# First tiles by half features, interleaved loads, and first place for the up-projection's reads of PSUM, in a fused attention and feed-forward kernel

**Chip, cores, metric.** One core of one Trainium2 chip. The time is device microseconds of one execution; all runs here are in the fast state. A profile's span is 1.7 to 1.8 us shorter than the time of the same run, so spans are compared with spans and times with times.

## The reference

```python
h  = x + A(layernorm(x))          # x: 2048 x 1024, bf16
h2 = h + B(layernorm(h))
# A: 32 heads of 32; four segments of 512 tokens, one after the other
#    causal softmax attention inside the segment, plus a linear memory
#    (phi(q) M) / (phi(q) z) of the earlier segments, mixed by sigmoid(beta); then @ wo
# B: (silu(x @ w1) * (x @ w3)) @ w2, with 3584 hidden features
```

## The kernel before

The program builds some thousands of operations with costs and dependencies; a list scheduler in it then fixes one order per engine. Each operation has a class (`cls`, lower goes first), and a table SHIFT, tuned beforehand by search, nudges the operations of each unit. Weights stream through two buffers for each of `w1b` and `w3b`, so a load can start only when the last matmul that reads its buffer is done.

The parts that the change and the argument touch are the sixteen warm-up matmuls, the normalisation of the first four 128-token tiles (`ln_act` on ScalarE for tile 1, `ln` on VectorE for the others), the first projections, and the three reads of an up-projection's PSUM banks (`sg`, `t1`, `hm`):

```python
    def constants(self):
        P = self.pool_op
        i = self.ident[:, :]
        w = self.oT[0][:, 4, :]
        self.dve_op(lambda e: e.memset(w, 0.0), 300.0, [], [w], 0)
        gr = self.dense_group()
        wl = self.oT[0][:, 4, 0:128]
        self.mms(gr, [(lambda gr: self.bank(gr), wl, w, True, True, 512)] * 16, 0, split=16)
        # ... [cut: identity, masks, ones]

    def ln_act(self, k, src, dst):

        self.g.stage()
        sm, nm, sq = (self.lnst[:, k, i:i + 1] for i in range(3))
        junk = self.oT[0][:, 0:2, :].rearrange("p a b -> p (a b)")
        G = self.g
        G.op("act", act_ns(1024), lambda e, gr: [e.activation(junk, src, AF.Copy, accum_out=sm)],
             reads=[src], writes=[junk, sm], cls=1)
        self.act(nm, sm, AF.Copy, 190.0, cls=1, scale=-1.0 / 1024)
        G.op("act", act_ns(1024, 1), lambda e, gr: [e.activation(
            junk, src, AF.Square, bias=nm, accum_out=sq)], reads=[src, nm], writes=[junk, sq],
            cls=1)
        ve, rs = self.lnve[:, k:k + 1], self.rstd[:, k:k + 1]
        mh = self.mhalf[:, :]
        self.pool_op(lambda e: e.tensor_scalar(ve, sq, 1.0 / 1024, self.EPS, op0=ALU.mult,
                                               op1=ALU.add), 1, [sq], [ve], 0)
        self.pool_op(lambda e: e.tensor_tensor(rs, ve, mh, op=ALU.pow), 190, [ve, mh], [rs], 0)
        self.dve_op(lambda e: e.tensor_scalar(dst, src, nm, rs, op0=ALU.add, op1=ALU.mult),
                    540.0, [src, nm, rs], [dst], 0, port=True)

    def ln(self, k, src, dst, cls):

        self.g.stage()
        st = self.lnst[:, k, :]
        mv = self.lnmv[:, k, :]
        for c in range(2):
            a, b = self.lnst[:, k, 6 * c:6 * c + 6], src[:, c * 512:(c + 1) * 512]
            self.dve_op(lambda e, a=a, b=b: e.bn_stats(a, b), 630.0, [b], [a], cls - 1)
        st2 = self.lnst[:, k, :].rearrange("p (a b) -> p a b", a=2)
        self.dve_op(lambda e: e.bn_aggr(mv, st2), 200.0, [st2], [mv], cls - 1)
        ve, rs = self.lnve[:, k:k + 1], self.rstd[:, k:k + 1]
        var, mean = self.lnmv[:, k, 1:2], self.lnmv[:, k, 0:1]
        mh = self.mhalf[:, :]
        self.pool_op(lambda e: e.tensor_scalar(ve, var, self.EPS, None, op0=ALU.add), 1,
                     [var], [ve], 0)
        self.pool_op(lambda e: e.tensor_tensor(rs, ve, mh, op=ALU.pow), 190, [ve, mh], [rs], 0)
        self.dve_op(lambda e: e.tensor_scalar(dst, src, mean, rs, op0=ALU.subtract,
                                              op1=ALU.mult), 540.0, [src, mean, rs], [dst],
                    0 if k < 4 else cls, port=True)

    def ln1(self, s):
        for i in range(4):
            t = 4 * s + i
            x = self.xs[t % 4][:, :]
            self.g.dma(x, self.x2d[t * 128:(t + 1) * 128, :], cls=0 if s == 0 else 2)
            if t == 1:
                self.ln_act(t, x, x)
            else:
                self.ln(t, x, x, 2 if s == 0 else 4 + s)
            if s:
                self.g.dma_t(self.xnT[s][:, :, i * 128:(i + 1) * 128], x, 3)
                continue
            gr = Group([(6,), (7,), (4,), (5,)], safe=True)
            self.transposes(gr, [(c * 128, self.xs[t % 4][:, c * 128:(c + 1) * 128])
                                 for c in range(8)], 2 if s == 0 else 4)
            out = self.xnT[s][:, :, i * 128:(i + 1) * 128]
            self.evac(gr, out, 1024, lambda b: b.rearrange("p (k n) -> p k n", k=8), cls=1,
                      bf=True)

    def first_half(self):


        (wq, sq), (wk, sk), (wv, sv) = (self.weights(kind, 0) for kind in "qkv")
        self.g.dma(wq[:, :, 0:256], sq[:, :, 0:256], cls=1)
        self.g.dma(wk[:, :, 0:256], sk[:, :, 0:256], cls=1)
        self.g.dma(wq[:, :, 256:512], sq[:, :, 256:512], cls=1)
        self.g.dma(wk[:, :, 256:512], sk[:, :, 256:512], cls=1)
        self.g.dma(wv[:, :, :], sv, cls=1)
        x = self.xnT[0]
        work = [(w, i, Group([(6,), (7,), (4,), (5,)], safe=True))
                for w in (wq, wk) for i in range(2)]
        for c0 in range(0, 512, 128):
            for w, i, gr in work:
                self.g.stage()
                self.mms(gr, [(lambda gr, c0=c0: self.bank(gr, 0, 128, c0),
                               w[:, c, i * 128:(i + 1) * 128], x[:, c, c0:c0 + 128],
                               c == 0, c == 7, 128) for c in range(8)], 5, split=8, eager=True)
        for w, i, gr in work:
            self.g.stage()
            out = (self.qT if w is wq else self.kT)[0][:, i, :]
            self.evac(gr, out, 512, lambda b: b, cls=1)
        # ... [cut: copies of q and k, the second half, v]

    # ... in ffn_up, for each 128 columns and each 512 tokens:
                for gr, w in ((gg, w1), (gu, w3)):
                    self.mms(gr, [(lambda gr: self.bank(gr),
                                   w[:, c, jj * 128:(jj + 1) * 128], hT[:, c, :],
                                   c == 0, c == 7, 512) for c in range(8)], 7)
                self.g.op("act", act_ns(512), lambda e, gr, sg=sg: [e.activation(
                    sg, self.bank(gr), AF.Tanh, scale=0.5)], writes=[sg], cls=2, group=gg)
                self.g.op("dve", dve_ns(512), lambda e, gr, sg=sg, t1=t1: [
                    e.scalar_tensor_tensor(t1, sg, 1.0, self.bank(gr), op0=ALU.add,
                                           op1=ALU.mult)], reads=[sg], writes=[t1], cls=2,
                    group=gg)
                dst = self.hm[fc][:, tc * 512:(tc + 1) * 512]
                self.g.op("dve", dve_ns(512), lambda e, gr, t1=t1, dst=dst: [
                    e.scalar_tensor_tensor(dst, t1, 0.5, self.bank(gr), op0=ALU.mult,
                                           op1=ALU.mult)], reads=[t1], writes=[dst], cls=2,
                    group=gu)
```

The softmax here doesn't subtract the row's maximum and nothing guards it: scores larger than these inputs give would overflow.

## Time and profile before

| | before |
|---|---|
| time, median of 3 runs | 906.06 us (905.48 to 906.42) |
| span of the profiled run | 905.0 us (that run took 906.68) |
| TensorE busy | 98% |
| VectorE, ScalarE, GpSimd busy | 46%, 32%, 20% |

Two rows of the page in forty slices of 22.6 us each (busy tenths), for the engine and the transfers that the change touches:

```profile
DVE  4586657789676566643353321211343333431111
DMA  7949852564731267722342321013123222301110
```

Counting slices from 0, VectorE reaches nine tenths only in slice 9 (204 to 226 us), and the DMA engines in slices 1 and 3. Neither is a bound on average; what matters is where TensorE waits for one of them. The rest of the page is read in the prediction. A caution for every count of TensorE: this trace has 5476 matmul records beside 5564 weight loads, about one in sixty missing. Sums over the whole span are corrected for that below.

### The profile page before, as it was taken

What the parts mean: (1) busy time and instruction counts of PE and PEld (TensorE: products, weight loads), DVE (VectorE), ACT (ScalarE), POOL (GpSimd) and SP (SyncE); (2) the same over time, 40 slices, a digit from 0 to 9 for tenths busy, and PEclk for the clock granted to TensorE, in tenths of its full rate; (3) what the DMA queues carried; (4) which work ended last, traced back from release to release, by engine and by line L of the source; (5) the groups of instructions that cost most, each with busy time, mean ns of one, the idle gap of its engine ahead of it and who ended that gap; (6) DMA issues with size and microseconds to landing.
All of it is one profiled execution on the core that took longest, in us unless ns stands there. A gap on an engine that the chain in (4) does not pass through costs nothing.

```text
span 905.0 us, 12909 instructions
## 1 busy us (share of the span) xinstructions
PE 890.9 (98%) x5476; PEld 409.4 (45%) x5564; DVE 420.5 (46%) x643; ACT 285.2 (32%) x299; POOL 179.9 (20%) x248
## 2 busy tenths in 40 slices
PE   8999999999999999999999999999999999999998
PEld 5444443434444344444444444444444444444445
DVE  4586657789676566643353321211343333431111
ACT  5768657685685721111111100000121111110000
POOL 2554538456374431000000000000000000000000
DMA  7949852564731267722342321013123222301110
GB/s 233 233 133 284 202 175 98 136 153 99 184 102 48 58 223 209 210 68 60 101 121 78 98 72 45 24 47 93 47 76 93 70 59 58 94 24 41 36 40 30
DMA packets 146473, 96.27 MB, mean 106 GB/s; under 512 B 45424, under 2 KB 133616, under 8 KB 146416
## 3 DMA queue, kind: packets, MB, share of 16 engines
q1 hardware_dynamic: 146416, 95.45, 37.9%
q8 instruction: 44, 0.72, 0.3%
q14 instruction: 13, 0.11, 0.0%
HBM read 76.55 MB, written 8.39 MB: 94 GB/s over the span
## 4 chain that ended last, share of the span: by engine, by line
PE 96%; DMA 2%; issue 1%; DVE 1%; ACT 0%; SPq 0%; POOL 0%; ACTq 0%
PE ps L706 89%; PE ps L1054 4%; PE ps L1009 3%; DMA wp<-in_A_wv_dram 1%; DMA xs<-in_A_x_dram 1%; DMA pkn<-pk 1%; ACT et L1021 0%; DVE hm L1179 0%; DVE t L1174 0%; SPq L297 0%; PE ps L718 0%; DVE oT L1125 0%; DVE R L1122 0%; DVE lnst L827 0%; ACT sg L1171 0%
## 5 line engine op out<-in xcount | busy, mean ns | idle before, releaser
L706 PE MATMUL ps<-hnT,w1b 128*128 128x512 bf16 x875 | 219.1, 379 | 1.3 <-issue 0.3
L706 PE MATMUL ps<-hnT,w3b 128*128 128x512 bf16 x882 | 216.7, 379 | 2.2 <-DVE hm L1179 1.5
L1171 ACT ACTIVATE sg<-ps 128x512 bf16<-128x512 f32 x112 | 66.9, 597 | 431.6 <-PE ps L706 431.6
L706 PE MATMUL ps<-w2b,hm 128*128 128x512 bf16 (+1 forms) x905 | 196.5, 372 | 1.0
L1174 DVE SCALAR_TENSOR_TENSOR t<-sg,ps 128x512 bf16<-128x512 bf16 x112 | 76.7, 685 | 194.3 <-ACT sg L1171 194.2
L1021 ACT ACTIVATE et<-ps 128x2048 bf16<-128x2048 f32 x80 | 149.9, 1874 | 31.2 <-PE ps L1009 30.9
L706 PEld LDWEIGHTS ps<-w2b,hm 128*128 128x128 bf16 x924 | 90.4, 98 | 103.3
L706 PEld LDWEIGHTS ps<-hnT,w3b 128*128 128x128 bf16 x896 | 87.2, 98 | 106.9 <-DMA w3b<-in_B_w_dram 1.9
L706 PEld LDWEIGHTS ps<-hnT,w1b 128*128 128x128 bf16 x896 | 87.1, 98 | 105.9 <-issue 8.2
L1030 POOL TENSOR_SCALAR_AFFINE_SELECT et<-et 128x512 bf16<-128x512 bf16 (+1 forms) x96 | 82.1, 862 | 93.0 <-ACT et L1021 93.0
L1179 DVE SCALAR_TENSOR_TENSOR hm<-t,ps 128x512 bf16<-128x512 bf16 x112 | 76.6, 686 | 46.0 <-PE ps L706 43.6
L1203 DVE TENSOR_TENSOR ob<-hr,ps 128x512 bf16<-128x512 bf16 (+1 forms) x33 | 22.1, 671 | 135.8 <-PE ps L706 135.8
L706 PE MATMUL ps<-wo,oT 128*128 128x512 bf16 x248 | 61.4, 379 | 0.7 <-issue 0.5
L706 PE MATMUL ps<-hnT,wp 128*128 128x512 bf16 x248 | 59.7, 380 | 0.9 <-issue 0.6
L706 PE MATMUL ps<-xnT,wp 128*128 128x512 bf16 (+1 forms) x344 | 59.6, 320 | 0.9 <-issue 0.6
L833 POOL TENSOR_SCALAR lnve<-lnmv 128x1 f32<-128x1 f32 x31 | 8.7, 284 | 167.8 <-DVE lnmv L829 167.7
L706 PEld LDWEIGHTS ps<-xnT,wp 128*128 128x128 bf16 x352 | 27.8, 98 | 25.0 <-issue 2.8
L706 PEld LDWEIGHTS ps<-wo,oT 128*128 128x128 bf16 x256 | 24.0, 98 | 29.3 <-issue 2.4
L706 PEld LDWEIGHTS ps<-hnT,wp 128*128 128x128 bf16 x256 | 23.5, 98 | 29.1 <-issue 3.6
L1108 DVE STREAM_TRANSPOSE R<-Rc 128x1024 f32<-128x1024 f32 (+1 forms) x32 | 35.0, 1099 | 0.3
L1009 PE MATMUL ps<-qT,kT 32*128 32x128 bf16 (+3 forms) x512 | 31.7, 301 | 0.3 <-ACT et L1021 0.2
L706 PE MATMUL ps<-wp,xnT 128*128 128x512 bf16 x122 | 30.3, 380 | 0.7 <-issue 0.6
(82 smaller groups left out, 567.5 us busy)
## 6 DMA issues: line engine op xcount, KB each, us to landing
w3b<-in_B_w_dram SPq DMA_DIRECT2D x28, 512.0 KB, 4.0
w1b<-in_B_w_dram SPq DMA_DIRECT2D x28, 512.0 KB, 3.8
wp<-in_A_wv_dram SPq DMA_DIRECT2D x8, 1024.0 KB, 7.3
wp<-in_A_wq_dram SPq DMA_DIRECT2D x7, 1024.0 KB, 5.3
wp<-in_A_wk_dram SPq DMA_DIRECT2D x7, 1024.0 KB, 5.4
w2b<-in_B_w_dram SPq DMA_DIRECT2D x7, 1024.0 KB, 7.2
xs<-in_A_x_dram SPq DMA_DIRECT2D x16, 256.0 KB, 5.4
h<-in_A_x_dram SPq DMA_DIRECT2D x16, 256.0 KB, 3.2
```

What stands on the lines that cost most here:

```text
L706: return [e.matmul(p[0](gr), p[1], p[2], start=p[3], stop=p[4]) for p in part]
L833: self.pool_op(lambda e: e.tensor_scalar(ve, var, self.EPS, None, op0=ALU.add), 1, [var], [ve], 0)
L1009: ins.append(e.matmul(self.bank(gr, j, 512 - 128 * kc, off), k[r, g0 + g, 128 * kc:128 * kc + 128], q[r, g0 + g, 128 * kc:512], start=True ...
L1021: return [e.activation(et[:, :, :], src, AF.Exp, scale=self.scale)]
L1030: self.pool_op(lambda e, v=v, pat=pat: e.affine_select(v, v, pattern=pat, compare_op=ALU.is_ge, fill=0.0, base=0, channel_multiplier=-1), ...
L1054: ins.append(e.matmul(self.ps[32 * j:32 * j + 32, b * 512 + 128 * kc:(b + 1) * 512], lhsT(i, kc, j), at[i, kc][:, j, :], start=kc == 0 and ...
L1108: sp = self.dve_op(lambda e, dst=dst, src=src: e.transpose(dst, src), dve_ns(512 * nr), [Rc[:, i, 0:nr, :]], [rs], 1)
L1171: self.g.op("act", act_ns(512), lambda e, gr, sg=sg: [e.activation(sg, self.bank(gr), AF.Tanh, scale=0.5)], writes=[sg], cls=2, group=gg)
L1174: e.scalar_tensor_tensor(t1, sg, 1.0, self.bank(gr), op0=ALU.add, op1=ALU.mult)], reads=[sg], writes=[t1], cls=2,
L1179: e.scalar_tensor_tensor(dst, t1, 0.5, self.bank(gr), op0=ALU.mult, op1=ALU.mult)], reads=[t1], writes=[dst], cls=2,
L1203: self.g.op("dve", dve_ns(n), lambda e, gr, hs=hs, ob=ob, n=n: [e.tensor_tensor(ob, hs, self.bank(gr, 0, n), op=ALU.add)], reads=[hs], wri ...
```

## The change

The intent: let TensorE start on real work earlier. Tile by tile, the normalisation, the transposes and the copies out of PSUM go by halves of 512 features, the copies on VectorE and ScalarE in turn; tiles 1 and 3 take their statistics on ScalarE, tiles 0 and 2 on VectorE; the first loads are interleaved (two tiles, half of wq, two tiles, half of wk). The three reads of the up-projection's banks get the highest class. The scheduler's costs are corrected and SHIFT is searched anew, so the order of everything moves.

```diff
[cut: SHIFT, the table of offsets and priorities of some 490 units, retuned as a whole]
@@ -563,7 +559,7 @@
 
 
 def pool_ns(n, inputs=1):
-    return 170.0 + n * (0.88 if inputs == 1 else 2.1)
+    return 210.0 + n * (0.88 if inputs == 1 else 2.1)
 
 
 def mm_ns(n):
@@ -753,15 +749,23 @@
             self.queues[b] = g
         return g
 
+    def warm(self, n, deps=()):
+
+        w = self.oT[0][:, 4, :]
+        gr = Group([(3,)])
+        o = self.mms(gr, [(lambda gr: self.bank(gr), self.oT[0][:, 4, 0:128], w, True, True,
+                           512)] * n, 0, split=n)
+        o.cost["pe"] *= 2
+        for d in deps:
+            self.g.dep(o, d)
+
 
     def constants(self):
         P = self.pool_op
         i = self.ident[:, :]
         w = self.oT[0][:, 4, :]
         self.dve_op(lambda e: e.memset(w, 0.0), 300.0, [], [w], 0)
-        gr = self.dense_group()
-        wl = self.oT[0][:, 4, 0:128]
-        self.mms(gr, [(lambda gr: self.bank(gr), wl, w, True, True, 512)] * 16, 0, split=16)
+        self.warm(10)
         P(lambda e: e.memset(i, 1.0), 128, [], [i], 0)
@@ -797,64 +801,77 @@
         self.dve_op(lambda e: e.tensor_scalar(gc, gc, 0.5, 0.5, op0=ALU.mult, op1=ALU.add),
                     dve_ns(8), [gc], [gc], 3)
 
-    def ln_act(self, k, src, dst):
+    def ln_act(self, k, src):
+
 
         self.g.stage()
-        sm, nm, sq = (self.lnst[:, k, i:i + 1] for i in range(3))
+        sm, nm, sq, nb = (self.lnst[:, k, i:i + 1] for i in range(4))
         junk = self.oT[0][:, 0:2, :].rearrange("p a b -> p (a b)")
         G = self.g
-        G.op("act", act_ns(1024), lambda e, gr: [e.activation(junk, src, AF.Copy, accum_out=sm)],
-             reads=[src], writes=[junk, sm], cls=1)
-        self.act(nm, sm, AF.Copy, 190.0, cls=1, scale=-1.0 / 1024)
-        G.op("act", act_ns(1024, 1), lambda e, gr: [e.activation(
-            junk, src, AF.Square, bias=nm, accum_out=sq)], reads=[src, nm], writes=[junk, sq],
-            cls=1)
+        G.op("act", act_ns(1024) + 190, lambda e, gr: [e.activation(
+            junk, src, AF.Copy, accum_out=sm)], reads=[src], writes=[junk, sm], cls=1)
+        self.act(nb, sm, AF.Copy, 203.0, cls=1, scale=-1.0 / 32768)
+        G.op("act", act_ns(1024, 1) + 190, lambda e, gr: [e.activation(
+            junk, src, AF.Square, bias=nb, scale=1.0 / 32, accum_out=sq)], reads=[src, nb],
+            writes=[junk, sq], cls=1)
+        self.act(nm, sm, AF.Copy, 203.0, cls=1, scale=-1.0 / 1024)
+        return sq, nm, ALU.add
[cut: ln split into ln_stats and ln; the costs of POOL operations spelled out]
+    def first_tile(self, t):
+
+        x = self.xs[t][:, :]
+        var, mean, op = self.ln_act(t, x) if t % 2 else self.ln_stats(
+            t, x, 1, (self.applied,) if t else ())
+        rs = self.rstd[:, t:t + 1]
+        ve, mh = self.lnve[:, t:t + 1], self.mhalf[:, :]
+        self.dve_op(lambda e: e.tensor_scalar(ve, var, self.EPS, None, op0=ALU.add), 70.0, [var],
+                    [ve], 0)
+        self.g.op("pool", 570.0, lambda e, gr: [e.tensor_tensor(rs, ve, mh, op=ALU.pow)],
+                  reads=[ve, mh], writes=[rs], cls=0)
+        for b in range(2):
+            xb = self.xs[t][:, 512 * b:512 * b + 512]
+            self.applied = self.dve_op(lambda e, xb=xb: e.tensor_scalar(xb, xb, mean, rs, op0=op,
+                                                                     op1=ALU.mult),
+                                       290.0, [xb, mean, rs], [xb], 0, port=True)
+            gr = Group([(0,), (1,), (2,)], safe=True)
+            self.transposes(gr, [(c * 128, self.xs[t][:, 512 * b + c * 128:512 * b + c * 128 + 128])
+                                 for c in range(4)], 2)
+            out = self.xnT[0][:, 4 * b:4 * b + 4, t * 128:(t + 1) * 128]
+            if t == 0 and b:
+                self.warm(1, [self.g.ops[-1]])
+            self.evac(gr, out, 512, lambda v: v[:, 0:512].rearrange("p (k n) -> p k n", k=4),
+                      cls=1, bf=True, engs=("dve", "act"))
 
     def ln1(self, s):
         for i in range(4):
             t = 4 * s + i
-            x = self.xs[t % 4][:, :]
-            self.g.dma(x, self.x2d[t * 128:(t + 1) * 128, :], cls=0 if s == 0 else 2)
-            if t == 1:
-                self.ln_act(t, x, x)
-            else:
-                self.ln(t, x, x, 2 if s == 0 else 4 + s)
-            if s:
-                self.g.dma_t(self.xnT[s][:, :, i * 128:(i + 1) * 128], x, 3)
-                continue
-            gr = Group([(6,), (7,), (4,), (5,)], safe=True)
-            self.transposes(gr, [(c * 128, self.xs[t % 4][:, c * 128:(c + 1) * 128])
-                                 for c in range(8)], 2 if s == 0 else 4)
-            out = self.xnT[s][:, :, i * 128:(i + 1) * 128]
-            self.evac(gr, out, 1024, lambda b: b.rearrange("p (k n) -> p k n", k=8), cls=1,
-                      bf=True)
+            x = self.xs[i][:, :]
[cut]
@@ -896,20 +913,25 @@
 
 
         (wq, sq), (wk, sk), (wv, sv) = (self.weights(kind, 0) for kind in "qkv")
-        self.g.dma(wq[:, :, 0:256], sq[:, :, 0:256], cls=1)
-        self.g.dma(wk[:, :, 0:256], sk[:, :, 0:256], cls=1)
-        self.g.dma(wq[:, :, 256:512], sq[:, :, 256:512], cls=1)
-        self.g.dma(wk[:, :, 256:512], sk[:, :, 256:512], cls=1)
-        self.g.dma(wv[:, :, :], sv, cls=1)
+        dma = self.g.dma
+        loads = [(self.xs[t][:, :], self.x2d[t * 128:(t + 1) * 128, :]) for t in range(4)]
+        loads.insert(2, (wq[:, :, 0:256], sq[:, :, 0:256]))
+        loads.insert(5, (wk[:, :, 0:256], sk[:, :, 0:256]))
+        loads += [(wq[:, :, 256:512], sq[:, :, 256:512]), (wk[:, :, 256:512], sk[:, :, 256:512]),
+                  (wv[:, :, :], sv)]
+        for out, in_ in loads:
+            dma(out, in_, cls=0)
+        for t in range(4):
+            self.first_tile(t)
         x = self.xnT[0]
-        work = [(w, i, Group([(6,), (7,), (4,), (5,)], safe=True))
+        work = [(w, i, Group([(5,), (6,), (7,), (4,)], safe=True))
                 for w in (wq, wk) for i in range(2)]
         for c0 in range(0, 512, 128):
             for w, i, gr in work:
                 self.g.stage()
                 self.mms(gr, [(lambda gr, c0=c0: self.bank(gr, 0, 128, c0),
                                w[:, c, i * 128:(i + 1) * 128], x[:, c, c0:c0 + 128],
-                               c == 0, c == 7, 128) for c in range(8)], 5, split=8, eager=True)
+                               c == 0, c == 7, 128) for c in range(8)], 5, split=4, eager=True)
         for w, i, gr in work:
             self.g.stage()
             out = (self.qT if w is wq else self.kT)[0][:, i, :]
[cut: a POOL cost, and one transpose of the attention from class 1 to 2]
@@ -1169,15 +1191,15 @@
                                    w[:, c, jj * 128:(jj + 1) * 128], hT[:, c, :],
                                    c == 0, c == 7, 512) for c in range(8)], 7)
                 self.g.op("act", act_ns(512), lambda e, gr, sg=sg: [e.activation(
-                    sg, self.bank(gr), AF.Tanh, scale=0.5)], writes=[sg], cls=2, group=gg)
+                    sg, self.bank(gr), AF.Tanh, scale=0.5)], writes=[sg], cls=0, group=gg)
                 self.g.op("dve", dve_ns(512), lambda e, gr, sg=sg, t1=t1: [
                     e.scalar_tensor_tensor(t1, sg, 1.0, self.bank(gr), op0=ALU.add,
-                                           op1=ALU.mult)], reads=[sg], writes=[t1], cls=2,
+                                           op1=ALU.mult)], reads=[sg], writes=[t1], cls=0,
                     group=gg)
                 dst = self.hm[fc][:, tc * 512:(tc + 1) * 512]
                 self.g.op("dve", dve_ns(512), lambda e, gr, t1=t1, dst=dst: [
                     e.scalar_tensor_tensor(dst, t1, 0.5, self.bank(gr), op0=ALU.mult,
-                                           op1=ALU.mult)], reads=[t1], writes=[dst], cls=2,
+                                           op1=ALU.mult)], reads=[t1], writes=[dst], cls=0,
                     group=gu)
 
     def ffn_down(self, blk):
[cut: the call of ln1(0) removed]
```

## The prediction

> **What bounds the kernel now.** I read four views in this order: the page (who is busy), the waits of TensorE, the timeline of the places where TensorE stood still, and the landing times of the first loads.
>
> The page first: the busy line, the busy row of PE by slices, and the head of the chain that ended last.
>
> ```profile
> PE 890.9 (98%) x5476; PEld 409.4 (45%) x5564; DVE 420.5 (46%) x643; ACT 285.2 (32%) x299; POOL 179.9 (20%) x248
> ...
> PE   8999999999999999999999999999999999999998
> ...
> PE 96%; DMA 2%; issue 1%; DVE 1%; ACT 0%; SPq 0%; POOL 0%; ACTq 0%
> ```
>
> TensorE is the bound everywhere except in the first slice and the last. Busy is not the same as peak, so I checked the pitch: the starts of the 128x512 matmuls are 0.216 us apart from 322.9 us to 902.4 us, in pieces of 10.79 us, with one record missing in each piece and only 0.37 us lost in all. That stretch is the feed-forward block, and nothing in it can be gained. What is left is the opening, a few waits in the attention stretch (20 to 322 us), and the tail after the last matmul (905.0 - 902.4 = 2.6 us, which the change doesn't touch).
>
> The second view, waits of TensorE from 13.5 to 322 us (columns: total us, times, longest):
>
> ```profile
> PE ps L706 <- issue: 2.5, 16, 0.2
> PE ps L706 <- DVE hm L1179: 1.5, 1, 1.5
> PE ps L706 <- DMA wp<-in_A_wv_dram: 0.3, 1, 0.3
> PE ps L706 <- DMA pkn<-pk: 0.2, 1, 0.2
> PE ps L706 <- DVE R L1122: 0.2, 1, 0.2
> PE ps L1009 <- ACT et L1021: 0.2, 1, 0.2
> ```
>
> "issue" is the gap at a switch between full and tiled matmuls, about 0.1 us each, and there are 80 score blocks before and after. One wait stands out, 1.5 us for the second read of an up-projection's PSUM bank. The timeline of VectorE at that place:
>
> ```profile
> 300.09 0.75 DVE L1122 SCALAR_TENSOR_TENSOR R<-ps,gcol,R 128x512 f32<-128x512 f32 x1
> 300.88 0.85 DVE L1125 TENSOR_TENSOR oT<-R 128x512 bf16<-128x512 f32 x1
> 301.65 0.68 DVE L1174 SCALAR_TENSOR_TENSOR t<-sg,ps 128x512 bf16<-128x512 bf16 x1
> 302.26 0.70 DVE L927 TENSOR_SCALAR phe<-phe 128x1024 bf16<-128x1024 bf16 x1
> 302.89 0.67 DVE L1179 SCALAR_TENSOR_TENSOR hm<-t,ps 128x512 bf16<-128x512 bf16 x1
> ```
>
> TensorE finished its score block at 302.04 and had no free bank until hm was written at 303.57. VectorE did oT and phe first, which free no bank.
>
> The third view, the opening on TensorE (start, length, what):
>
> ```profile
> 1.24 6.22 PE L706 MATMUL ps<-oT 128*128 128x512 bf16 x16 [1.24 <-DVE oT L761]
> 7.36 0.62 PE L718 MATMUL ps<-ident,xs 128*128 128x128 bf16 x8
> 9.23 0.62 PE L718 MATMUL ps<-ident,xs 128*128 128x128 bf16 x8 [1.25 <-DVE xs L817]
> 9.68 1.06 PE L706 MATMUL ps<-xnT,wp 128*128 128x128 bf16 x16
> 10.89 0.62 PE L718 MATMUL ps<-ident,xs 128*128 128x128 bf16 x8
> 11.35 1.95 PE L706 MATMUL ps<-xnT,wp 128*128 128x128 bf16 x32
> 13.13 0.61 PE L718 MATMUL ps<-ident,xs 128*128 128x128 bf16 x8
> ```
>
> Sixteen warm-up matmuls, then four tiles transposed one by one, then a stream. To turn the opening into one number I subtract from a time in the stream the useful work done by then (0.056 us per 128-wide, 0.216 per 512-wide matmul). The first score block starts at 19.86, after 32 transposes, 112 narrow and 12 wide matmuls: 1.79 + 6.25 + 2.59 = 10.63. So the opening costs 9.2 us.
>
> The fourth view, landing events of the loads, last of the 16 parts: x tiles at 3.44, 4.46, 6.13 and 7.41 us, first half of wq 9.15, first half of wk 10.82, second halves 12.51 and 14.16, wv 18.48. The transfers run at 290 GB/s without a pause, so a load's landing goes with the bytes queued before it.
>
> **What the Trainium skill says.** "TensorE: Matmul & The Clock Gate", Part 1: the array is at half clock until it has been busy for a window of about 3.4 us, and falls back after an idle one; 426.7 ns per cold wide matmul against 215.7 warm. The trace agrees: 0.427 us apart until about 6.4 us, 0.216 afterwards. "DMA: Bandwidth & Descriptors", "Issuing engines are not separate DMA queues" and "Queues, rings and completion order": on each DMA engine descriptors are taken in ring order. The trace agrees: landings are in issue order. So interleaving loads moves arrivals, not the sum. "VectorE: DVE Perf Modes", the errata section: each instruction has a fixed latency, so halves cost more than a whole. The trace has bf16 128x1024 applications at 0.54 us; no half of it is in this trace.
>
> **The change part by part.**
> 1. Up-projection reads of PSUM get the highest priority. In the stretch above, 0.70 us (phe) and 0.85 us (oT) no longer come before the reads. The wait was 1.5; I book -1.4. In the dense stretch one gap of 0.15 us goes: -0.1. The rest of that stretch has no gap to save, though its VectorE and ScalarE rows all change.
> 2. The opening. Warm-up falls from 16 to 10 plus 1, ending near 1.24 + 10 x 0.427 = 5.5 us. This saves nothing itself: the first tile wasn't ready by then. Loads now go x0, x1, wq half, x2, x3, wk half; by bytes wq half lands near 7.4, x2 near 8.3, x3 near 9.15 and wk half again at 10.82. Tile 0: landed 3.44, statistics to 4.75, aggregate to 5.1, the added epsilon on VectorE to 5.3, power on POOL (0.57) to 6.0, halves applied at 6.3 and 6.6, transposed and copied by about 7.4 and 8.0. First real matmuls near 7.5 instead of 9.68. But only the 16 with wq and tile 0 can go. Tile 1 has its first copy on ScalarE, behind the sum of tile 3, which waits for x3 at 9.15: 1.06 + 0.19 + 0.60 gives 11.0. At 11.1 TensorE has done 16 transposes and 16 matmuls, 1.8 us of work, so the opening stands at 9.3. From there 40 narrow matmuls are ready (2.2 us, to 13.3). On VectorE the epsilon of tile 3 stands before the application of tile 2, and waits for ScalarE's square: 11.05 + two small operations of 0.2 + 1.15 + 0.19 gives 12.85. Tile 2 is then applied by 13.35 and 13.65, tile 3 by 14.1 and 14.4, and their copies end by 16.0 while TensorE has old work between. I find 0.25 us of holes. Opening: 9.5 against 9.2, +0.3. The early start is eaten by a longer idle time, because wk half lands no earlier.
> 3. The retuned order of everything. Work on TensorE is the same but for the five warm-up matmuls; one more block of tiled attention matmuls is split, two switches, +0.2. The space between score blocks must hold one exp (1.87 us) and its handshakes. Before, three spaces have 2.37 us of matmuls or less, and two of them cost 0.2 each. The new order has eight such, +0.6 if they cost 0.1 to 0.2. Against it, the old waits for wv (0.48), for pkn (0.3) and the like, about 1 us in all, sit at places that a new order shuffles: -0.3.
> Sum: -1.5 + 0.3 + 0.2 + 0.6 - 0.3 = -0.7. That the costs in the scheduler's tables were brought near the trace (power 0.57, epsilon, the accumulator read 0.19) speaks for a somewhat better order than my count, so I take -1.3: 904.8 us.
>
> **The rivals.**
> A. The opening really gets shorter, by 1.5 to 2 us (to 902.5 to 903.5). For: first matmuls 2 us earlier, epsilon off POOL, copies on two engines. Against: wk half at 10.82 caps what can be done, and the copy of tile 1 stands behind a landing.
> B. The clock stays cold. With busy time ending at 5.5 and tile 0 at 6.4, the window that ends near 6.4 is about three quarters busy. If that isn't enough, the 128-wide work goes at 0.107 until the next window, 9.8 or 13.2: up to +1.5 us, to 907. For: the removed matmuls were the ones that made that window full. Against: one warm-up was put back, and TensorE is waiting for data then anyway.
> C. A new wait takes the place of the removed one: VectorE serves the up-projection first and is late with the attention's eviction or a normalised tile, 1 to 3 us, to 906 to 908. For: VectorE is 9.09 us busy of 10 from 290 to 300. Against: four reads of 0.69 us only.
>
> **Range and chances.** All of the gain must come out of some 9 us of opening and 4 us of waits; even all waits and 2 us of opening are 6 us, 0.7%. So over 2% either way is next to impossible. A: 0.3, B or C: 0.3, near my sum: 0.4. Predicted 904.8, 8 in 10 between 902.3 and 907.4; faster by 2% 0.01, within 0.98, slower 0.01.
>
> **What would show it.** First real matmul near 7.5 us; then TensorE idle until about 11; opening (as computed above) 9.5. No wait of TensorE for hm in the attention stretch. Dense stretch unchanged at 0.216. Waits for exp somewhat more in number. Wide matmuls at 0.427 or transposes 0.107 apart after 6.5 us would show B. If the opening is below 8.5, or a single new wait exceeds 1 us, my working is wrong there.

## The result

| | before | changed |
|---|---|---|
| time, median of 6 runs each, same chip | 905.85 us (905.48 to 906.77) | 905.81 us (905.46 to 905.98) |
| ratio of the means | | 0.9997, 95% interval 0.9985 to 1.0010 |
| span of the profiled run | 905.0 us | 904.1 us |

A ratio here is the mean time of one kernel's fast runs over the mean of the other's of the same rounds, so not quite the ratio of the medians. The change is worth nothing that can be measured. (Before's profiled run was one of its slower ones, so the 0.9 us between the spans flatters the change.)

The page of the changed kernel, the busy line and the head of the chain that ended last:

```profile
PE 897.7 (99%) x5559; PEld 409.7 (45%) x5559; DVE 427.7 (47%) x653; ACT 284.5 (31%) x303; POOL 186.7 (21%) x246
...
PE 97%; DMA 2%; DVE 0%; issue 0%; ACT 0%; POOL 0%; SPq 0%
```

PE's row of forty slices is the same as before's to the digit: the two places where TensorE can gain are still the first slice and single waits. The busy time rose by 6.8 us only because this trace lacks no matmul record: b_prio below, which has before's order and lacks none either, has 897.7 us too.

To see where time went I split each span in three: the opening (as the prediction computes it: start of the first score block minus the useful work before it), the waits of TensorE after that, and the rest (matmuls at full pitch, the switches between matmuls on the whole array and those on a part of it, the tail).

| us | before | changed |
|---|---|---|
| opening | 9.2 | 9.17 |
| waits after it | 2.8 | 1.62 |
| rest | 893.0 | 893.3 |
| sum, the span | 905.0 | 904.1 |

The waits of TensorE in the changed kernel (total us, times, longest), for the attention stretch from 13.5 to 322 us and, after the dots, from 322 us to the end:

```profile
PE ps L702 <- DMA wp<-in_A_wq_dram: 0.2, 1, 0.2
...
PE ps L702 <- DMA w3b<-in_B_w_dram: 0.9, 2, 0.5
```

The 1.5 us wait at 302 us is gone, as are the waits for wv and pkn. (Before's rows for "issue" and R are gone too, but they were no waits: b_prio, the same order with all records, has neither.) But the feed-forward stretch, in which before lost 0.37 us in all, now has two waits for a load of w3b. The timeline of TensorE at these (start, length, what, and in brackets the idle time before it):

```profile
484.44 1.90 PE L702 MATMUL ps<-hnT,w3b 128*128 128x512 bf16 x8 [0.39 <-DMA w3b<-in_B_w_dram]
...
627.57 1.90 PE L702 MATMUL ps<-hnT,w3b 128*128 128x512 bf16 x8 [0.51 <-DMA w3b<-in_B_w_dram]
```

Measured from start to start and less the pitch, they cost 0.55 and 0.67 us; the wait for wq at 27 us costs 0.39. That is 1.6 us, all three for DMA.

**The opening.** TensorE in the changed kernel:

```profile
6.61 1.01 PE L714 MATMUL ps<-ident,xs 128*128 128x128 bf16 x8 [0.93 <-DVE xs L856]
...
7.84 1.91 PE L702 MATMUL ps<-xnT,wp 128*128 128x128 bf16 x16
9.55 0.83 PE L714 MATMUL ps<-ident,xs 128*128 128x128 bf16 x8
10.84 2.41 PE L702 MATMUL ps<-xnT,wp 128*128 128x128 bf16 x40 [0.47 <-ACT xnT L725]
```

The first projection starts at 7.84 instead of 9.68 us. Behind its sixteen matmuls and the transposes of tile 1 TensorE has nothing until 10.84, while before took up tile 2 at 10.89. The sixteen matmuls from 7.84 take 1.91 us: they run 0.107 us apart, at half clock. The reason for the gap is on ScalarE:

```profile
8.93 1.06 ACT L811 ACTIVATE oT<-xs 128x1024 bf16<-128x1024 bf16 x1 [0.67 <-DMA xs<-in_A_x_dram]
9.89 0.19 ACT L811 ACTIVATION_READ_ACCUMULATOR oT<-xs 128x1 f32 x1
10.19 0.60 ACT L725 ACTIVATE xnT<-ps 128x512 bf16<-128x512 bf16 x1
```

The sum of tile 3 waits for its load, which landed at 8.91; the copy of tile 1, which TensorE needs, stands behind it and ends at 10.79.

**A second look at before.** The prediction put the 1.5 us at 302 us on VectorE's `hm`. Two lines of before's page, side by side, should have stopped me: the same matmuls, once as matmuls and once as weight loads (busy us, mean ns; then idle time before them and what ended most of it):

```profile
L706 PE MATMUL ps<-hnT,w3b 128*128 128x512 bf16 x882 | 216.7, 379 | 2.2 <-DVE hm L1179 1.5
...
L706 PEld LDWEIGHTS ps<-hnT,w3b 128*128 128x128 bf16 x896 | 87.2, 98 | 106.9 <-DMA w3b<-in_B_w_dram 1.9
```

And the timeline of weight loads at the place:

```profile
301.71 0.10 PEld L1009 LDWEIGHTS ps<-qT,kT 32*128 32x128 bf16 x4 [0.42 <-ACT sg L1171]
303.39 0.55 PEld L706 LDWEIGHTS ps<-hnT,w3b 128*128 128x128 bf16 x4 [1.58 <-DMA w3b<-in_B_w_dram]
```

The weight load waited 1.58 us for the DMA of w3b. That load was issued at 297.49; fifteen of its sixteen parts had landed by 302.14, the last at 303.35, 0.04 us before the weights were read. `hm` was still being written then (until 303.56); by the program's dependencies the bank of these matmuls had been freed by R, which ended at 300.84. Why, then, does the matmul line name `hm`?

```profile
303.62 0.81 PE L706 MATMUL ps<-hnT,w3b 128*128 128x512 bf16 x3 [1.51 <-DVE hm L1179]
```

It has x3 where there are four weight loads. The record of the first matmul is one of those missing from this trace; it would stand at 303.40 (303.62 less a pitch of 0.216), before the end of `hm`. What the line calls the first matmul is the second, and the last event before that one was `hm`. The weight load line names what held TensorE. The Trainium skill, page "DMA: Bandwidth & Descriptors", section "Why a DMA increments its semaphore by 16 and not by 1", says that the parts run on engines that finish independently and that only the full count means that all data has landed. The trace agrees: one part of sixteen, 1.21 us behind the others, held TensorE.

That left two theories for the wait at 302 us. **D (DMA), "Theory B" in the recorded expectations:** the wait is for the load; the priority of the reads does nothing, and the changed kernel's gain there was paid back at two other loads. **V (VectorE), the prediction's, "Theory A" there:** the reads, done late, hold the bank. And two for the opening: either the landing of the first loads sets it, or what the code can change does (clock, copy order, ScalarE).

### The profile page after: what moved, and what is told of

It is laid out like the page before. It is cut to its first block, busy times and chain, and to the rows that moved or that the text cites. A ratio compares the mean times of both kernels' runs of the same rounds, so it can differ in the third digit from the quotient of the medians.

```text
span 904.1 us, 12979 instructions
## 1 busy us (share of the span) xinstructions
PE 897.7 (99%) x5559; PEld 409.7 (45%) x5559; DVE 427.7 (47%) x653; ACT 284.5 (31%) x303; POOL 186.7 (21%) x246
## 4 chain that ended last, share of the span: by engine, by line
PE 97%; DMA 2%; DVE 0%; issue 0%; ACT 0%; POOL 0%; SPq 0%
PE ps L702 90%; PE ps L1076 4%; PE ps L1031 3%; DMA w3b<-in_B_w_dram 1%; DMA wp<-in_A_wq_dram 1%; DMA xs<-in_A_x_dram 0%; PE ps L714 0%; DVE lnst L825 0%; ACT xnT L725 0%; POOL rstd L852 0%; DVE xs L856 0%; DVE ob L1225 0%; DVE lnmv L828 0%; DVE lnve L850 0%; DVE blkmask L788 0%
## 5 line engine op out<-in xcount | busy, mean ns | idle before, releaser
L702 PE MATMUL ps<-hnT,w3b 128*128 128x512 bf16 x896 | 219.0, 379 | 0.9 <-DMA w3b<-in_B_w_dram 0.9
L1052 POOL TENSOR_SCALAR_AFFINE_SELECT et<-et 128x512 bf16<-128x512 bf16 x96 | 88.4, 927 | 81.7 <-ACT et L1043 81.6
L702 PE MATMUL ps<-wo,oT 128*128 128x512 bf16 x256 | 63.9, 380 | 0.0
L702 PE MATMUL ps<-xnT,wp 128*128 128x512 bf16 (+1 forms) x352 | 62.5, 326 | 0.7 <-ACT xnT L725 0.5
L702 PE MATMUL ps<-hnT,wp 128*128 128x512 bf16 x256 | 62.6, 380 | 0.0
L835 POOL TENSOR_SCALAR lnve<-lnmv 128x1 f32<-128x1 f32 x28 | 6.3, 228 | 150.8 <-DVE lnmv L828 150.7
L1135 POOL TENSOR_TENSOR R<-Nsb,R 128x512 f32<-128x512 f32 x20 | 26.7, 1341 | 34.9 <-DVE R L1130 26.7
L1165 DVE TENSOR_TENSOR h<-h,ps 128x512 bf16<-128x512 bf16 x32 | 21.9, 684 | 24.8 <-PE ps L702 24.7
```

Of the source, the lines that this page charges most:

```text
L702: return [e.matmul(p[0](gr), p[1], p[2], start=p[3], stop=p[4]) for p in part]
L1052: self.pool_op(lambda e, v=v, pat=pat: e.affine_select(v, v, pattern=pat, compare_op=ALU.is_ge, fill=0.0, base=0, channel_multiplier=-1), ...
L1135: self.either(lambda e, o1=o1, Ns=Ns, R0=R0: e.tensor_tensor(o1, Ns, R0, op=ALU.mult), 512, 2, [Ns, R0], [o1], 2)
L1165: self.g.op("dve", dve_ns(512), lambda e, gr, hs=hs: [e.tensor_tensor(hs, hs, self.bank(gr), op=ALU.add)], reads=[hs], writes=[hs], cls=1, ...
```

## The experiments

In every kernel below whose edit is a move, the scheduler's order is frozen and replayed, so that one move reshuffles nothing else. All gave correct results. "Before" ran beside them, with medians of 905.97, 906.83, 906.54 and 905.88 us in the four batches, which is the scatter between chips and calls: only ratios are compared across batches.

### b_swap: before, with the bank's reads ahead of the other VectorE work

```diff
  VectorE near 301 us, frozen order of before
  R
- oT
- t
- phe
- hm
+ t
+ hm
+ oT
+ phe
```

> The kernel before with its order of instructions frozen and one edit: near 302 us VectorE does the two reads of the up-projection (t, then hm) ahead of oT and phe. Theory A (the 1.5 us wait of TensorE is for the read hm, as the prediction had it): hm ends near 302.7 instead of 303.57, TensorE resumes near 302.8, the wait shrinks to about 0.7 us, span shorter by 0.8 us. Theory B (the wait is for the load of w3b, which landed at 303.35 in the trace of before, its 16 parts spread over 2.6 us; hm was only the last to come by the profile): TensorE resumes when w3b has landed, whatever VectorE does; where the load lands on time there is no wait at all; the edit itself is worth 0, time within 0.3 us of before.

Measured: 905.59 us, ratio 0.9996 (0.9984 to 1.0008). VectorE and then TensorE at the place:

```profile
301.47 0.69 DVE L1209 SCALAR_TENSOR_TENSOR hm<-t,ps 128x512 bf16<-128x512 bf16 x1
```

```profile
302.06 1.04 PE L736 MATMUL ps<-hnT,w3b 128*128 128x512 bf16 x4 [0.52 <-DMA w3b<-in_B_w_dram]
```

`hm` now starts 1.4 us earlier than in before (301.47 against 302.89; 0.85 of that against the score block ahead of it, 301.14 here and 301.71 there). The wait is still there, and now it bears its right name: w3b landed at 302.01 and TensorE went on at 302.06. `hm` itself ended at 302.16, after TensorE had gone on, so it did not hold the bank. The wait is shorter (0.52) because the last part of this load was less late (0.53 us behind the fifteenth, against 1.21), not because of VectorE; the next run shows that.

### b_prio: before, with the new classes alone

```diff
- sg: cls=2    t: cls=2    hm: cls=2
+ sg: cls=0    t: cls=0    hm: cls=0
```

> The kernel before with only the priority of the three up-projection reads raised, as in the change; the scheduler then places later work anew. Theory A: about -1.5 us in the profile, no TensorE wait over 1 us in the attention stretch. Theory B: the reads are worth nothing; the time stays within 0.7 us of before, and what waits TensorE has in the feed-forward stretch are for loads of w1 or w3.

Measured: 906.37 us, ratio 1.0007 (0.9992 to 1.0022). I compared the compiled order with before's: not one instruction moves on any engine. The priority change is a no-op in before's schedule, and this kernel is a repeat of before. In that repeat:

```profile
303.02 1.04 PE L706 MATMUL ps<-hnT,w3b 128*128 128x512 bf16 x4 [0.77 <-DMA w3b<-in_B_w_dram]
```

```profile
303.03 0.67 DVE L1179 SCALAR_TENSOR_TENSOR hm<-t,ps 128x512 bf16<-128x512 bf16 x1
```

TensorE went on at 303.02, before `hm` even began; w3b had landed at 302.97. With the same instructions the wait was 1.5 us in one run and 0.77 in another: it follows the load. Theory V is out, and D holds at this place.

### a_noprio: the changed kernel without the new classes

```diff
- sg: cls=0    t: cls=0    hm: cls=0
+ sg: cls=2    t: cls=2    hm: cls=2
```

> The changed kernel with the priority of the reads put back to what it was. Theory A: a wait for hm of about 1 us or more returns, +1 to +1.5 us. Theory B: within 0.7 us of the changed kernel, waits for loads of w3b of 0 to 1.3 us in all at other places.

Measured: 906.08 us, ratio to before 0.9997 (0.9985 to 1.0009), just the ratio of the whole change. The order differs from the changed kernel's in a few rows only (four operations of VectorE moved). No wait for `hm` came back; the waits of TensorE after 13.5 us are all loads:

```profile
PE ps L702 <- DMA w3b<-in_B_w_dram: 0.6, 2, 0.4
PE ps L702 <- DMA wp<-in_A_wq_dram: 0.3, 1, 0.3
```

So the wait at 302 us went because the new order issues that w3b at 296.46 and it landed at 300.11, ahead of its use, not because of the classes.

### a_warm16: the changed kernel with sixteen warm-up matmuls again

```diff
- self.warm(10)
+ self.warm(16)      # the cost in the scheduler left at that of 10, so the order stays
```

> The changed kernel with 16 warm-up matmuls emitted instead of 10, all else in the same order. Theory of the cold clock (rival B of the prediction, as seen in the trace after: narrow matmuls 0.107 us apart until about 9.9 us): they are 0.056 apart from about 6.6 us, the transposes of tile 1 end near 9.1 instead of 10.2. But the first copy of tile 1 waits on ScalarE behind the sum of tile 3 (landing at 8.9), so TensorE resumes at 10.8 all the same: opening within 0.2 us of 9.2, time within 0.4 us of the changed kernel. If the cold clock is what costs, the opening falls by 0.5 us or more.

Measured: 905.45 us, ratio 0.9989 (0.9977 to 1.0000). TensorE in the opening:

```profile
8.06 1.07 PE L702 MATMUL ps<-xnT,wp 128*128 128x128 bf16 x16 [0.22 <-DMA wp<-in_A_wq_dram]
...
11.10 2.41 PE L702 MATMUL ps<-xnT,wp 128*128 128x128 bf16 x40 [1.35 <-ACT xnT L725]
```

The sixteen projections run at full clock here, 1.07 us instead of 1.91, yet TensorE resumed at 11.10, later than the 10.84 of the changed kernel, because tile 3 landed later, at 9.39. In this run, then, the full clock bought no earlier start. In a_w3b2 below the projections from 8.1 us ran at half clock (0.107 us apart), and TensorE resumed 1.71 us after tile 3's landing, just as here. The opening was 9.43 (expected: within 0.2 of 9.2), and the small gain of the run lies elsewhere: 1.08 us of waits instead of 1.62. No edit touched those waits: the one at 627 us, 0.67 in the changed kernel, is absent here by chance.

### a_act: tile 1's copy ahead of tile 3's sum on ScalarE

```diff
  ScalarE
- sum of tile 3; copy of tile 1
+ copy of tile 1; sum of tile 3
```

> The changed kernel, order frozen, with one edit on ScalarE: the first copy of tile 1 goes ahead of the sum of tile 3. Theory of the landing behind the copy (the copy stood behind the sum, which waits for tile 3's load at 8.8 to 9.4 us): TensorE's first narrow matmul of tile 1 starts at about 9.6 to 10.4 instead of 10.5 to 11.1. After four of them the order asks for the half of wk, landing at 10.6 to 11.2, so a second wait takes the place of the first and the opening stays at 8.8 to 9.4, time within 0.5 us. Rival: the copy alone held the opening; then it falls to 8.5 or less.

Measured: 907.67 us, ratio 1.0008 (0.9996 to 1.0021); opening 10.24, span 906.6: both expectations (8.8 to 9.4, or 8.5 or less) failed. The copy came no earlier, since here the transposes of tile 1 were late (TensorE at half clock again, as in the changed kernel's profile). And tile 3's sum, now behind the copy, made a new hole:

```profile
14.15 0.40 PE L744 MATMUL ps<-ident,xs 128*128 128x128 bf16 x4 [0.65 <-DVE xs L886]
```

These are tile 2's transposes: on VectorE the epsilon of tile 3 stands ahead of tile 2's application and waits for ScalarE. Waits for wq at 29 us and for w3b at 487 and 630 us added up to 2.7 us in this run; they are the three loads that the changed kernel waits for, and the one at 487 us was later (1.39 us lost instead of 0.55).

### a_open: the opening taken apart by hand

```diff
+ sixteen warm-ups; copy of tile 1 ahead of the sum of tile 3 (ScalarE)
+ tile 1 with wq ahead of the matmuls with wk (TensorE)
+ epsilon of tile 3 behind the application of tile 2 (VectorE)
```

> The changed kernel, order frozen, with 16 warm-up matmuls, the ScalarE edit of a_act, all 16 wq matmuls of tile 1 ahead of those with wk on TensorE, and on VectorE the epsilon of tile 3 after the application of tile 2. By the durations of the trace: tile 1's matmuls from about 10.1, done by 11.0, wk's 32 by 12.8, tile 2 copied by about 13.6: opening 8.7 (8.3 to 9.0) against 9.2, time 0.3 to 0.8 us below the changed kernel. Rival: the loads set the opening whatever the order, and it stays within 0.2 of 9.2.

Measured: 905.95 us, ratio 0.9992 (0.9979 to 1.0006), opening 9.69: my expectation of 8.7 failed. TensorE did resume earlier, at 10.48, and the hole before tile 2 is gone, but another came before tile 3:

```profile
14.51 0.38 PE L744 MATMUL ps<-ident,xs 128*128 128x128 bf16 x4 [0.73 <-DVE xs L888]
```

Sum, square, power and two applications follow tile 3's landing in any order. In these two profiles, whichever went first on ScalarE, the other was late.

### a_w3b and a_best: slack for the late loads, first try

```diff
  a_w3b, changed kernel
+ 479 us: the last reader of the w3b buffer seven blocks of four matmuls earlier, its load ahead of two others
+ 627 us: the block that needs the late w3b two blocks later
+ 27 us: a block with wk ahead of the block that needs wq
  a_best: a_w3b and a_open together
```

> The changed kernel, order frozen, with three edits at its waits for loads: the last use of a w3b buffer 7 groups of four matmuls earlier and its load first of three (wait at 484 us), a matmul group that needs a fresh w3b two groups later (wait at 627), and a wk group ahead of a wq group (wait at 26.9). Theory: late loads are what is left; the waits of 0.29 to 0.55, 0.56 to 0.67 and 0.39 to 0.51 us go, no other wait grows beyond 0.2 us, time 1.0 to 1.6 us below the changed kernel in the profile. Rival: the waits move to the next load, and the time stays within 0.4 us.

> a_open and a_w3b together. If both hold: 1.3 to 2.2 us below the changed kernel and the kernel before, near 904.0 us where those give about 905.8; ratio to before about 0.998. If the waits only move: within 0.5 us of the others.

Measured: a_w3b 907.02 us, ratio 1.0001 (0.9988 to 1.0013); a_best 906.98, ratio 1.0005 (0.9993 to 1.0018): neither gain came. The load waits at 484 and 627 us went, and bank waits came in their place:

```profile
PE ps L732 <- DVE hm L1231: 0.9, 2, 0.5
```

The block that had been moved away from 479 us was what gave VectorE time to empty the next bank: 0.62 us lost at 480 us, and 0.66 at 627. The wait at 480 us is 0.62 in all four kernels with this move (a_w3b, a_best, a_w3b2, a_best2), where waits for loads differ from run to run. Here, and not at 302 us, is the wait that the prediction had in mind. a_best has both tries and both new holes, and came out no better.

### a_xfirst: the four x tiles ahead of wq

```diff
- loads: x0, x1, wq half, x2, x3, wk half
+ loads: x0, x1, x2, x3, wq half, wk half
+ sixteen warm-ups; tile 2's statistics not held for tile 1; tile 1 with wq ahead of wk
```

> The changed kernel with its order frozen, and the opening taken apart by hand: the four x tiles load before the first half of wq, sixteen warm-up matmuls, the statistics of tile 2 on VectorE no longer held until tile 1 is applied, tile 1's copy on ScalarE left behind the sum of tile 3 (whose tile now lands near 7.4 us instead of 8.9), and the matmuls of tile 1 with wq before those with wk. Theory (the opening of the changed kernel is set by tile 3's load through ScalarE, not by wk): x3 lands near 7.4, first real matmuls wait for wq to about 9.1, then no hole over 0.3 us; opening 8.2 to 8.6 us against 9.17 of the changed kernel, span 903.2 to 904.0 with its other waits (about 1.6 us) unchanged, ratio to before 0.998 to 0.9995. Rival (the bytes set it: the order of loads only moves the hole, as the two openings before this one did): opening 9.1 to 9.9, ratio 1.000 to 1.001.

Measured: 906.60 us, ratio 1.0002 (0.9989 to 1.0014); the rival held. Tile 3 landed at 7.46 as hoped, and wq at 9.23:

```profile
9.28 1.07 PE L732 MATMUL ps<-xnT,wp 128*128 128x128 bf16 x16 [1.23 <-DMA wp<-in_A_wq_dram]
```

The hole has moved in front of the first projection, and the opening is 9.78. Together with the other runs this shows what sets the opening. "Last" is the landing of the later of tile 3 and the first half of wq:

| kernel | last to land | opening | difference |
|---|---|---|---|
| b_swap | wq 8.71 | 8.65 | -0.06 |
| b_prio | wq 8.96 | 9.20 | 0.24 |
| before | wq 9.15 | 9.2 | 0.05 |
| a_w3b3 (below) | tile 3 8.08 | 8.20 | 0.12 |
| a_w3b | tile 3 8.45 | 8.52 | 0.07 |
| a_noprio | tile 3 8.80 | 8.83 | 0.03 |
| changed | tile 3 8.91 | 9.17 | 0.26 |
| a_w3b2 (below) | tile 3 9.35 | 9.57 | 0.22 |
| a_warm16 | tile 3 9.39 | 9.43 | 0.04 |
| a_best2 (below) | wq 8.60 | 9.15 | 0.55 |
| a_xfirst | wq 9.23 | 9.78 | 0.55 |
| a_open | tile 3 9.00 | 9.69 | 0.69 |
| a_act | tile 3 8.31 | 10.24 | 1.93 |
| a_best | tile 3 7.63 | 9.86 | 2.23 |

In both tuned orders, before's and the changed one, the opening equals the landing of the first 1.5 MB (four tiles and half of wq) to within 0.3 us, whichever piece comes last. That is an agreement of two numbers; which load holds TensorE has to be read from the chain of waits. The landing itself moves from run to run: with the changed kernel's order of loads tile 3 landed between 7.63 and 9.39 us in nine profiles. By the difference in the table my own orders of the opening all do worse than both. Six kernels have the changed kernel's order there (itself, a_noprio, a_warm16, a_w3b, a_w3b2, a_w3b3): TensorE resumed 1.71 us after tile 3 landed in five of them, and 1.93 after it in the changed kernel's own profile. So there tile 3 decides, through ScalarE.

In before's order it isn't wq, though wq lands last. The chain that ended last (start, length, what), in before's profile:

```profile
2.17 5.24 DMA xs<-in_A_x_dram
...
7.43 0.71 DVE lnst L827 x2
...
8.64 0.53 DVE xs L817
```

A statistic on VectorE waits for tile 3, which lands at 7.41; tile 1's application stands behind it, and TensorE waits for that until 9.23. In b_swap and b_prio the chain starts at tile 2's landing (5.78 and 6.33) and takes the same way; wq is in none of the three. The first projections started 0.39 to 0.69 us after wq had landed. So in both orders the landing of an x tile, and the work on VectorE or ScalarE behind it, sets the opening; wq does so only in a_xfirst and a_best2, where the projections start 0.05 us after it.

### a_w3b2, a_best2, a_w3b3: slack for the late loads, second try

```diff
  a_w3b2, changed kernel
+ 479 us as in a_w3b; 627 us: one block later, not two; the move at 27 us left out
  a_best2: a_w3b2 and a_xfirst together
  a_w3b3, changed kernel, no load moved; two neighbouring blocks exchanged at each place
+ 484 us: the four matmuls that need the late w3b behind four that have their weights
+ 627 us: one block later
```

> The changed kernel with its order frozen and only the two late w3b loads of the feed-forward stretch given slack: at 484 us the w3b matmuls move behind the ones that have their weights and the load moves ahead of two others; at 627 us one block of matmuls moves behind the next. The fourth move of the earlier try (the wq at 27 us), which made a new wait of 0.3 us, is left out, and the block at 627 moves by one place, not two, since two places ran into an unread bank. Theory (the two holes are the loads, and slack removes them): no wait over 0.2 us at 478 to 490 and 620 to 635, losses after the opening 0.4 to 0.9 us against 1.62, span 903.0 to 903.8 with an opening of 9.2. Rival (each move only exposes the next load or bank): a wait of 0.4 to 0.7 us at another place in these stretches, span 904 or more.

> Both edits together: the opening with the four x tiles first and the slack for the two w3b loads. If both theories hold, opening 8.2 to 8.6 and losses after it 0.4 to 0.9: span 902.2 to 903.2 us, ratio to before 0.997 to 0.9985. If both rivals hold, span 904 to 905.5 and ratio 0.9995 to 1.001.

> The changed kernel with its order frozen and two moves on TensorE only: at 484 us the first four matmuls that need the late w3b go behind four that have their weights, and at 627 us one block goes behind the next. No load is moved and no other work is put earlier, so the banks are freed as in the changed kernel (the move before this one took four matmuls from ahead of an unread bank and waited 0.62 us there). Theory (the 1.2 us that the changed kernel lost in the feed-forward stretch are two loads with no slack, and a slack of one block, 0.86 us, is enough): no wait over 0.2 us between 470 and 640 us, losses after the opening 0.1 to 0.5 us against 1.62, span 902.5 to 903.5 with an opening of 8.8 to 9.6, ratio to before 0.997 to 0.9990. Rival (a straggling part of a load is as late as the slack, or a bank is in the way again): a wait of 0.3 us or more stays at 484 or 627 us, span over 903.7.

| | time, us | ratio to before | span | opening | waits after it |
|---|---|---|---|---|---|
| a_w3b2 | 905.09 | 0.9986 (0.9974 to 0.9999) | 903.5 | 9.57 | 0.62 |
| a_best2 | 906.05 | 0.9998 (0.9985 to 1.0012) | 903.7 | 9.15 | 1.28 |
| a_w3b3 | 904.66 | 0.9989 (0.9976 to 1.0003) | 902.1 | 8.20 | 0.6 |

(a_w3b3's trace again lacks one matmul record in sixty; its last two columns are corrected for that.) In a_w3b2 both load waits are gone, and what is left is the bank at 480 us:

```profile
481.04 2.75 PE L732 MATMUL ps<-hnT,w1b 128*128 128x512 bf16 x12 [0.45 <-DVE hm L1231]
```

In a_w3b3 that one is gone too: at 484 us TensorE runs through the stretch from w1b to w3b with no idle time noted,

```profile
482.22 3.62 PE L732 MATMUL ps<-hnT,w3b 128*128 128x512 bf16 x16
```

and its only waits of note are 0.41 for wq at 26 us and 0.14 at 395 us. Its waits are 1.0 us shorter than the changed kernel's, as theory D asks. Not all of that is the two moves: in this run the two loads landed 5.32 and 4.40 us after their issue (5.49 and 4.75 in the changed kernel's profile), and I estimate from these landings that the changed order would have waited 0.4 us for the first and 0.3 for the second. (The same estimate gives 0.29 and 0.56 for a_noprio, which measured 0.29 and 0.56.) So the slack saved some 0.7 us here. The wait at 484 us is there in all six kernels that leave this place alone (0.29 to 1.39 us), the one at 627 in only three of them. Of the 2.0 us between this span and the changed kernel's, the other 1.0 us is the opening, where this run's loads landed early: luck, since nothing of the opening was edited. The expectations held for the waits between 470 and 640 us and for the ratio; span and opening came out lower than expected, by that luck. For a_w3b2 the rival held in part (the wait at 481 us), and a_best2 came out at its rivals' ratio. The ratio of a_w3b3, 0.9989, is the size that 1 us of 906 should have, but its interval still touches 1. That of a_w3b2 ends at 0.9999, which among twelve kernels tried can be chance. These two are the best versions found; neither is shown to beat the other.

## Why the prediction was right or wrong

The time predicted, 904.8 us, was 1.0 us low, inside the range, and the class was right. But the range also held before's own time, and "no change" would have been nearer. The prediction's own sum, -0.7, gave 905.4; the last 0.6 us, taken on trust in the better costs of the scheduler, led away from the result. The largest term of the sum is one that failed, so that the total is near is partly luck. The steps:

**Step 1 failed: the reads of PSUM.** "VectorE did oT and phe first, which free no bank" is true and had no effect. The step booked -1.4 us for the wait at 302 us on the word of one row whose first record was missing; b_prio shows that the new classes move no instruction of before, and b_swap that doing the reads first leaves TensorE waiting for the same load. The term of the priority is 0 in before's order and not measurable in the new one (a_noprio and the whole change have the same ratio, 0.9997). The wait did vanish, by the new order's earlier load, so the check named beforehand ("no wait of TensorE for hm") was met for a reason that wasn't mine. A check that two causes pass tells them apart from nothing.

**Step 1, second part, and "dense stretch unchanged": wrong.** I read a stretch with 0.37 us lost as one where nothing could be lost either. The new order put 1.2 us of load waits there. This has the size of rival C (the prediction gave it 1 to 3 us), but it came through DMA and not through VectorE.

**Step 2, the opening: mechanism right, size off by 0.3.** First projections at 7.84 us (7.5 predicted), then idle until 10.84 (11.1), behind tile 3's landing and sum on ScalarE: so it happened. (In between there are tile 1's transposes, which leave 0.47 us idle just before 10.84.) The opening is 9.17 and not 9.5; the 0.25 us of holes at tiles 2 and 3 that I added do not appear in this order. Tile 3 landed at 8.91 and not at 9.15, and the two small operations on ScalarE overlapped the operations before and after them, so that the epsilon of tile 3 came at 12.19 and not at 12.85 (the terms of that sum give 12.79). The holes do appear, as 0.65 to 0.9 us, as soon as the copy goes first (a_act, a_open). The sentence that the early start is eaten "because wk half lands no earlier" named the wrong load: tile 3 decides here. The half of wk landed at 10.69, 0.15 us before TensorE resumed, so it is the next in line.

**Step 3, the order: sum near, parts off.** One more split block was to cost 0.2 and the rest rose by 0.33. The +0.6 for waits on exp didn't come: no score block of the changed kernel starts more than 0.01 us later than the switch takes. Before had one such wait, 0.22 at 38.7 us, and not two: at 187.4 us a record is missing (seven matmuls beside eight weight loads). The -0.3 for the small waits of the attention stretch was too small: the waits for wv (0.48), pkn (0.27) and exp went, and one for wq (0.39) came.

**A reading that doesn't stand.** The row "issue: 2.5, 16" was read as the gaps at switches. b_prio has before's order and no such row: these 2.5 us too come from missing records, as does the row for R. So the "4 us of waits" of the range were 2.8 (table above). (A slip without weight: the score block before the wait ended at 302.10, not 302.04.)

**Rivals.** A failed: an earlier start by 1.8 us gave no shorter opening. B came true in part and was nearly free: the changed kernel's profile has the clock at half until about 9.9 us, while a_noprio and a_w3b, with the same ten warm-ups, were at full clock by 6.8. The most I can put on it is the 0.2 us between 1.93 and 1.71 in the opening; that this is the clock is argued, not shown, and a_w3b2 had half the clock from 8.1 us and 1.71. The skill's page "TensorE: Matmul & The Clock Gate", Part 1, calls the warm-up "run-variable", and these runs agree.

**In sum:** -0.03 in the opening, -1.2 in the waits, +0.3 in the rest between the two profiles, -0.9 in all. Of the -1.2, before's share is inflated: at 302 us the weight loads waited 1.58 us in its profile, but 0.81 and 1.06 in the two others of the same order. With the mean of the three orders' waits (2.8, 1.98 and 2.39: 2.4) the gain would be about 0.5 us, less than the scatter of single runs, and the medians show 0.04. What remains open is how much of a landing's lateness is chance: I saw it vary and did not control it.

## What to carry to other kernels

When a matmul's wait is put on the engine that freed a bank, look at its weight load's own wait, at the landing of the load, and at the count of matmuls in the row before you believe it: where a record is missing, the row names what came last before the next one. Before you value a priority change, compare the compiled orders; if no instruction moves, it is worth nothing. Here, with TensorE 98% busy, reordering moved waits from one load to the next; a block of slack ahead of a late load's first use took its wait away, where a faster reader did nothing. But a block moved earlier may be the one that hid the emptying of the next bank. And a load that lands last need not be the one that is waited for: follow the chain.

## What the Trainium skill lacked or had wrong

- "DMA: Bandwidth & Descriptors", "Why a DMA increments its semaphore by 16 and not by 1": right that the sixteen parts end independently; it has no size for it. Over the 54 loads of w1b and w3b after 280 us in before's trace, the last part came a median of 0.07 us behind the fifteenth, 0.42 at the ninetieth percentile, 1.45 at most, and over 0.5 in 5 of 54; in the changed kernel's 52 loads 0.05, 0.20 and 1.21.
- The same page gives nothing on how much the first loads of a kernel vary: with one order of loads, tile 3 landed between 7.63 and 9.39 us in nine profiles.
- "Perfetto Trace Analysis", "Optimization Strategy", advises to find the semaphore or semaphores that a gap waits on. It has no warning that matmul records can be missing and that the wait is then put on another semaphore: at 302 us in before, 1.51 us on `hm` in the row with x3 and 1.58 us on w3b in the row of its four weight loads; 5476 matmul records stand beside 5564 weight loads.
- "VectorE: DVE Perf Modes", the errata section: its cycle formula for sources in SBUF gives an estimate of 0.19 us for a 128x512 bf16 application at four elements a cycle and 0.33 us for 128x1024; the traces have 0.41 (0.74 for two, which overlap) and 0.53 to 0.55. The page itself says that the fixed part is larger; here halving one application cost 0.2 us more of VectorE.
